# A decode kernel (cached attention plus a ReLU feed-forward) whose two last products are turned: activations stationary in four column tiles of the array, output stored as rows

## The chip, the cores and the metric

One core of one Trainium2 chip. The metric is the device time of one execution in microseconds (us); each kernel is run several times, and compared with runs of the kernel before made in the same sitting. "Faster", "same" and "slower" have a line at 2%.

TensorE multiplies matrices, VectorE and ScalarE work on vectors, GpSimd fills and copies small things, SyncE here only issues transfers. In the profile they are PE (PEld for weight loads), DVE, ACT, POOL and SP; a trailing q (SPq, ACTq) is the sequencer of that engine, where the issues of transfers stand.

## The reference

```python
# x [2,1,512]; k_cache, v_cache [2,32,8192,128]; wq [512,4096]; wo [4096,512]
# w1 [512,1792]; w2 [1792,512]; all bf16
xn  = layernorm(x)
q   = (xn @ wq), 32 heads of 128
p   = softmax(q k^T / sqrt(128)) over the 8192 cached keys
att = (p v, heads joined) @ wo
ffn = max(xn @ w1, 0) @ w2
out = x + att + ffn                      # [2,1,512]
```

The caches are 2 x 32 x 8192 x 128 x 2 bytes = 134 MB each. Two rows of 512 numbers come out. There is little to compute and much to read.

## The kernel before

The loop runs over 32 pairs of heads: keys are transposed on TensorE, scores and weighted sums follow, and transfers of the next keys and values wait for the buffers to come free. The change leaves that loop alone. It concerns FFN2 (the product with w2, ahead of the loop), wo and the end. First the views of the accumulators:

```python
y = Sc[1][0:Bsz, :]                                      # FFN2: 2 x 512
fin = ot[0][:, 0:KT * Bsz].rearrange("p (b c) -> p c b", c=KT)   # 128 x (2 x 4)
```

TensorE computes `out = lhsT.T @ rhs`; `lhsT` is stationary and is loaded first, `rhs` moves through. FFN2 has the hidden activations stationary (two columns) and streams 512 columns of w2:

```python
for j in range(FJ):                                      # 16
    half = slice(0, HP if j >= FA else P)
    i = pe.matmul(y, lhsT=hT[half, j, :], rhs=w2_sb[half, j, :],
                  start=(j == 0), stop=(j == FJ - 1))
...
v.tensor_tensor(out=ys[:], in0=y, in1=xsb[:], op=ALU.add)   # FFN2 + x
```

After the loop, x + FFN2 is put into the accumulator `fin` by four small fp32 matmuls; wo then has its weights stationary, 128 x 128 at a time, and two moving columns. The result lies transposed (features on partitions), so it is cast, transposed on TensorE, copied and stored as eight adjacent rows of 128:

```python
for k in range(KT):
    pe.matmul(fin[:, k, :], lhsT=ys[:, k * P:(k + 1) * P], rhs=ident2[:],
              start=(k == 0), stop=False)
... # last pair, normalisation, OX = attention output in the order of wo
for c in range(NC):                                      # wo arrives in five pieces
    pe.wait_ge(dW[c], 16)
    for j in range(cuts[c], cuts[c + 1]):                # 32 in all
        for k in range(KT):                              # 4
            t = pe.matmul(fin[:, k, :], lhsT=wo_sb[:, j, k * P:(k + 1) * P],
                          rhs=OX[:, j, :], ...)
pe.transpose(tp[1][0:Bsz * KT, 0, :], yT[:]..., identb[:])
...
v.tensor_copy(yT[:], ...)                                # ahead of the transpose
v.tensor_copy(osb[:], tp[1][0:Bsz * KT, 0, :])           # behind it
sp.dma_start(out.rearrange("b s (c p) -> (b s c) p", p=P), osb[:])
```

## Time and profile before

| | before |
|---|---|
| time | 661.26 us, median of 3 runs (661.19 to 661.27) |
| span of the profiled run | 659.3 us |
| bytes read | 280.5 MB, 425 GB/s over the span |
| last piece of wo has landed | 655.54 us |
| store issued | 656.76 us |

A piece of wo has landed when the last increment of its semaphore has arrived (a semaphore is the counter that tells when a transfer is complete). The span counts from the first to the last instruction. Times in the views are us from its start. A row of the timeline has the start, the duration, the engine, the line, the operation, output<-input, the shapes and a count; the bracket at the end says how long the engine had stood idle and what ended that. The last part of the chain of work that ended last, with start, duration and piece, shows where the transfers stop being the limit:

```profile
625.89 29.65 DMA w_sb<-in_A_wo_dram
655.54 0.05 issue
655.58 0.39 PE ot L412 x8
655.97 0.02 issue
655.99 0.18 DVE yT L519
656.17 0.04 issue
656.21 0.28 PE tp L421
```

Until 655.54 us the chain is one long transfer; all that computation can lengthen or shorten at this end are the steps below it.

### The profile page before, as it was taken

The page shows a single profiled execution, that of the slowest core. Times are in us where ns is not written, and L with a number is a line of the kernel's source. Part 1 is how long each engine was busy: PE and PEld are TensorE (multiplying, and loading weights), DVE is VectorE, ACT ScalarE, POOL GpSimd, SP SyncE. Part 2 cuts the span into 40 slices and gives each one's busy share as a digit, 9 for nine tenths or more (in the row PEclk, how much of TensorE's full clock was granted, in tenths as well). Part 3 has the DMA queues.
Part 4 walks back from the last instruction along what each step waited for, and adds up shares of the span by engine and source line. Part 5 has one row for each costly group of instructions (what it writes and reads, how often), then busy time and mean ns, then how long its engine had stood idle before and what let it go on. Part 6 is the DMA issues. An engine that isn't in the chain of part 4 may idle for free.

```text
span 659.3 us, 26888 instructions
## 1 busy us (share of the span) xinstructions
PE 562.9 (85%) x12747; PEld 538.3 (82%) x12747; DVE 253.4 (38%) x437; ACT 255.9 (39%) x403; POOL 9.0 (1%) x46
## 2 busy tenths in 40 slices
PE   2998899988799787889888788979787998788796
PEld 0488898988799787888888788978787988788795
DVE  1054344433344343334434334434333444334341
ACT  1043444444334433344343434434243444334340
POOL 1000000000000000000000000000000000000000
PEclk9798899989989898999889899979899989889998
DMA  8999999999999999999999999999999999999996
GB/s 363 447 417 437 419 437 429 431 439 423 439 423 435 431 429 439 423 439 423 435 435 427 441 419 439 427 431 437 425 441 419 439 427 431 437 425 441 421 426 266
DMA packets 10670, 280.66 MB, mean 426 GB/s; under 512 B 1250, under 2 KB 1252, under 8 KB 1828
## 3 DMA queue, kind: packets, MB, share of 16 engines
q1 hardware_dynamic: 10656, 280.50, 99.1%
q8 instruction: 9, 0.15, 0.1%
q14 instruction: 1, 0.01, 0.0%
q10 hardware_dynamic: 4, 0.00, 0.0%
HBM read 280.50 MB, written 0.00 MB: 425 GB/s over the span
## 4 chain that ended last, share of the span: by engine, by line
DMA 56%; PE 39%; ACT 2%; issue 1%; SPq 0%; DVE 0%; ACTq 0%
DMA ks<-in_A_k_cache_dram 50%; PE tp L300 21%; PE Sc L307 11%; DMA w_sb<-in_A_wo_dram 4%; PE ot L320 4%; DMA vs<-in_A_wq_dram 2%; ACT kT L427 2%; PE ot L252 1%; PE Sc L285 1%; PE ot L266 1%; ACT L427 1%; SPq L199 0%; PE Sc L355 0%; PE Sc L358 0%; SPq L194 0%
## 5 line engine op out<-in xcount | busy, mean ns | idle before, releaser
L300 PE MATMUL tp<-identb,ks 128*128 128x128 bf16 x4096 | 326.0, 229 | 68.2 <-DMA ks<-in_A_k_cache_dram 67.4
L427 DVE COPY kT<-tp 128x1024 bf16<-128x1024 bf16 x320 | 219.8, 691 | 325.1 <-PE tp L300 324.9
L300 PEld LDWEIGHTS tp<-identb,ks 128*128 128x128 bf16 x4096 | 257.2, 103 | 72.1 <-DMA ks<-in_A_k_cache_dram 70.5
L427 ACT COPY kT<-tp 128x1024 bf16<-128x1024 bf16 x192 | 194.3, 1012 | 233.4 <-PE tp L300 233.4
L307 PE MATMUL Sc<-q,kT 128*128 128x64 bf16 x4096 | 216.6, 196 | 4.6 <-ACT kT L427 4.6
L307 PEld LDWEIGHTS Sc<-q,kT 128*128 128x128 bf16 x4096 | 178.8, 100 | 7.9 <-ACT kT L427 7.8
L320 PE MATMUL ot<-prm,vs 128*128 128x64 bf16 x4224 | 156.1, 192 | 4.7 <-issue 4.7
L320 PEld LDWEIGHTS ot<-prm,vs 128*128 128x128 bf16 x4224 | 139.0, 97 | 7.5 <-issue 4.9
L542 ACT COPY nm<-Sc 128x2 f32<-128x2 f32 x32 | 5.1, 160 | 118.4 <-PE Sc L358 118.4
L546 ACT ACTIVATE prm<-Sc,nm 64x128 bf16<-64x128 f32 x64 | 25.6, 401 | 4.3
L483 DVE TENSOR_REDUCE mcol<-Sc 64x1 bf16<-64x128 f32 x64 | 18.6, 291 | 17.6 <-PE Sc L307 17.2
L427 ACT ACT_TABLE_LOAD x16 | 20.5, 1283 | 2.2
L252 PE MATMUL ot<-vs,xz 128*16 128x512 bf16 x32 | 9.3, 462 | 8.8 <-DMA vs<-in_A_wq_dram 8.8
L534 ACT COPY OTf<-ot 128x2 f32 x32 | 5.1, 160 | 27.3 <-PE ot L320 27.3
L488 DVE TENSOR_REDUCE mx<-Sc 1x2 bf16<-1x128 bf16 x32 | 8.9, 279 | 16.9 <-PE Sc L355 16.9
L252 PEld LDWEIGHTS ot<-vs,xz 128*16 128x16 bf16 x32 | 3.3, 103 | 14.4 <-issue 12.0
L237 POOL COPY q<-qb 128x2 bf16<-128x2 bf16 x32 | 5.9, 187 | 590.8 <-PE Sc L307 567.5
L546 ACT ACTIVATION_READ_ACCUMULATOR prm<-Sc,nm x64 | 11.8, 185 | 0.0
L457 DVE TENSOR_SCALAR qs<-ot 16x512 bf16<-16x512 f32 x1 | 0.7, 678 | 17.9 <-PE ot L252 17.9
L355 PE MATMUL Sc<-identb,mcol 128*1 128x128 bf16 x32 | 7.0, 217 | 0.0
L285 PE MATMUL Sc<-w_sb,hT 128*2 128x512 bf16 (+1 forms) x16 | 6.0, 544 | 0.1
L358 PE MATMUL Sc<-mx,onesb 1*128 1x2 bf16 x32 | 5.5, 172 | 0.0
(56 smaller groups left out, 38.6 us busy)
## 6 DMA issues: line engine op xcount, KB each, us to landing
ks<-in_A_k_cache_dram SPq DMA_DIRECT2D x32, 4096.0 KB, 26.7
vs<-in_A_v_cache_dram SPq DMA_DIRECT2D x31, 4096.0 KB, 31.3
vs<-in_A_wq_dram SPq DMA_DIRECT2D x1, 4096.0 KB, 12.3
vs<-in_A_v_cache_dram SPq DMA_DIRECT2D x2, 2048.0 KB, 20.0
w_sb<-in_B_w_dram SPq DMA_DIRECT2D x1, 1792.0 KB, 16.1
w_sb<-in_A_wo_dram SPq DMA_DIRECT2D x1, 1792.0 KB, 26.0
w_sb<-in_B_w_dram SPq DMA_DIRECT2D x1, 1536.0 KB, 19.3
w_sb<-in_A_wo_dram SPq DMA_DIRECT2D x1, 896.0 KB, 27.7
```

The source lines that it names most:

```text
L237: g.tensor_copy(q2[t % R][:], qb[:, 2 * t:2 * t + 2]).then_inc(sQ1, 1)
L252: i = pe.matmul(qp, lhsT=xz[:, kt, Z - g * Bsz:Z - g * Bsz + QG * Bsz], rhs=vs[1][:, (kt * QG + g) * 512:(kt * QG + g + 1) * 512], start=( ...
L266: i = pe.matmul(hp[0:HP if j >= FA else P, j, :], lhsT=w1_b[:, kt, j - FA, :] if j >= FA else w1_a[:, kt, j, :], rhs=xz[:, kt, Z:Z + Bsz], ...
L285: i = pe.matmul(y, lhsT=hT[half, j, :], rhs=w2_sb[half, j, :], start=(j == 0), stop=(j == FJ - 1),)
L300: t = pe.transpose(tp[e % 4][:, i, :], ks[r][:, kk * Dh:(kk + 1) * Dh], identb[:])
L307: t = pe.matmul(Sc[r][:, 2 * kk:2 * kk + 2 * REP], lhsT=kT[e % 4][:, i, :], rhs=rep(q2[r][:]), start=True, stop=True,)
L320: t = pe.matmul(ot[r][:, 0:2 * REP], lhsT=vs[r][:, kk * Dh:(kk + 1) * Dh], rhs=rep(prm[r][:, kk, :]), start=(kk == 0), stop=(kk == KB - 1),)
L355: pe.transpose(tr_of(r), mcol[r][:], identb[:]).then_inc(sT, 1)
L427: fn(kT[e % 4][:], tp[e % 4][:]).then_inc(kR[e], 1)
L483: m = v.tensor_reduce(out=mcol[i][half, :], in_=S_of(i)[half, :, u], axis=AX.X, op=ALU.max)
L488: v.tensor_reduce(out=mx[i][:], in_=tr_of(i).rearrange("o (u m) -> o u m", u=2), axis=AX.X, op=ALU.max, negate=True,).then_inc(sX, 1)
L546: x = a.activation(out=prm[i][half, :, u], in_=S_of(i)[half, :, u], func=ACTF.Exp, bias=nm[i][half, u:u + 1], scale=1.0, accum_out=RS[half ...
```

## The change

The intent is to use the array better with only two activation rows. The activations, padded with zeros to 32 columns, become stationary; the weights move. The 128 columns of the array are used as four column tiles of 32, each of which takes its own quarter of the 512 output columns, so four matmuls can be in the array at once. The output then lies as rows: batch b, quarter c on partition 32c + b. The transpose and its two copies go, one addition remains, and the store becomes two stores of four rows, each 32 partitions from the next.

```diff
-    y = Sc[1][0:Bsz, :]
-    fin = ot[0][:, 0:KT * Bsz].rearrange("p (b c) -> p c b", c=KT)
+    y = Sc[1][:, 0:P]
+    fin = ot[0][:, 0:P]
+    def cols(ap, c):
+        return ap[c * CT:(c + 1) * CT, :]                # CT = 32
+    out_v = out.rearrange("b s (c p) -> (b s) c p", p=P)
+    def store(eng, b):
+        eng.dma_start(out_v[b], osb[b:b + (KT - 1) * CT + 1:CT, :]).then_inc(dO, 16)
 ...                                       # FFN2
-            i = pe.matmul(y, lhsT=hT[half, j, :], rhs=w2_sb[half, j, :], ...)
+            for c in range(KT):
+                pe.matmul(cols(y, c), lhsT=hT[half, j, :],
+                          rhs=w2_sb[half, j, c * P:(c + 1) * P], ...)
+        for c in range(KT):                # x joins by an identity
+            i = pe.matmul(cols(y, c), lhsT=identb[0:Bsz, 0:CT],
+                          rhs=xsb[:, c * P:(c + 1) * P], ...)
 ...                                       # after the loop
-        for k in range(KT):
-            pe.matmul(fin[:, k, :], lhsT=ys[:, k * P:(k + 1) * P], rhs=ident2[:], ...)
 ...                                       # wo
-                    t = pe.matmul(fin[:, k, :], lhsT=wo_sb[:, j, k * P:(k + 1) * P],
-                                  rhs=OX[:, j, :], ...)
+                    t = pe.matmul(cols(fin, k), lhsT=OX[:, j, :],
+                                  rhs=wo_sb[:, j, k * P:(k + 1) * P], ...)
-        pe.transpose(tp[1][0:Bsz * KT, 0, :], yT[:]..., identb[:])
 ...                                       # VectorE
-        v.tensor_copy(yT[:], ...)
-        v.tensor_copy(osb[:], tp[1][0:Bsz * KT, 0, :])
+        v.tensor_tensor(out=osb[:], in0=fin, in1=ys[:], op=ALU.add)
 ...                                       # SyncE, then ScalarE
-        sp.dma_start(out.rearrange("b s (c p) -> (b s c) p", p=P), osb[:])
+        store(sp, 0)
+        a.wait_ge(sE, 1)
+        for b in range(1, Bsz):
+            store(a, b)
```

Cut here: `OX` and `hT` become 32 columns wide and are zeroed at the start by GpSimd and VectorE.

## The prediction

> **What bounds the kernel now.** I read the page first: busy shares, the slices, then the bytes.
>
> ```profile
> PE 562.9 (85%) x12747; PEld 538.3 (82%) x12747; DVE 253.4 (38%) x437; ACT 255.9 (39%) x403; POOL 9.0 (1%) x46
> ...
> DMA  8999999999999999999999999999999999999996
> GB/s 363 447 417 437 419 437 429 431 439 423 439 423 435 431 429 439 423 439 423 435 435 427 441 419 439 427 431 437 425 441 419 439 427 431 437 425 441 421 426 266
> ...
> HBM read 280.50 MB, written 0.00 MB: 425 GB/s over the span
> ```
>
> The DMA row is at nine tenths in every slice but the first and last, and the GB/s row stands between 417 and 447 in between. TensorE looks busy (85%), but the view of waits says who waits for whom:
>
> ```profile
> PE tp L300 <- DMA ks<-in_A_k_cache_dram: 67.4, 26, 3.4
> ```
>
> In 26 of the 32 steps over a pair of heads TensorE waits for its block of keys, 67.4 us in all. So the loop is bound by 280.5 MB of reads, which the change does not touch; 280.5 MB over about 430 GB/s is an estimate of 652 us of transfer. What a change of arithmetic can reach is only (a) the end, after the last bytes have landed, and (b) the start, if TensorE became so late there that the transfers ran out of freed buffers. For (a) the timeline from 650.5 us on:
>
> ```profile
> 650.64 2.33 PEld L412 LDWEIGHTS ot<-OX,w_sb 128*128 128x128 bf16 x84 [0.44 <-DVE OX L515]
> 650.65 2.41 PE L412 MATMUL ot<-OX,w_sb 128*128 128x2 bf16 x84 [0.32 <-DVE OX L515]
> 654.09 0.71 PEld L412 LDWEIGHTS ot<-OX,w_sb 128*128 128x128 bf16 x24 [1.13 <-DMA w_sb<-in_A_wo_dram]
> ...
> 655.58 0.29 PEld L412 LDWEIGHTS ot<-OX,w_sb 128*128 128x128 bf16 x8 [0.18 <-DMA w_sb<-in_A_wo_dram]
> 655.99 0.17 DVE L519 CAST yT<-ot 128x8 bf16<-128x8 f32 x1 [5.40 <-PE ot L412]
> 656.21 0.08 PEld L421 LDWEIGHTS tp<-identb,yT 128*8 128x8 bf16 x1 [0.34 <-DVE yT L519]
> 656.21 0.27 PE L421 MATMUL tp<-identb,yT 128*8 128x128 bf16 x1 [0.26 <-DVE yT L519]
> 656.52 0.21 DVE L521 COPY osb<-tp 8x128 bf16<-8x128 bf16 x1 [0.36 <-PE tp L421]
> 656.76 0.32 SPq L201 DMA_DIRECT2D out_dram<-osb  x1
> ```
>
> Here 84 of the 128 matmuls of wo run at once, then TensorE waits for the later pieces of wo. The chain of the work that ended last has the last piece of wo landing at 655.54 us (its 29.65 us of DMA end there). After it come 0.39 us for the last eight matmuls, then cast, transpose, copy, and the store at 656.76; the span ends at 659.3. The path that the change can shorten is therefore 655.54 to 656.76, 1.22 us, plus whatever the store does in its last 2.54 us.
>
> **What the Trainium skill says.** "TensorEngine Tiling (Array Packing)", section Tiling Modes, says that different tiles load weights and multiply in parallel, and that a change of tiling mode drains the engine; its section Restrictions says that column tiling turns fast weight load off. No matmul of the kernel before writes fewer than all columns at an offset, so its trace neither confirms nor denies this. "TensorE: Matmul & The Clock Gate", section Part 3, gives 2.38 times for three column tiles of 32 columns with 512 moving columns. Its Part 1 has only two clocks on one core, half and full; this trace agrees: the stretches show 1.00 until 652 us and 0.50 from 653.1 to the end. "DMA: Bandwidth & Descriptors", section Issuing engines are not separate DMA queues, says that two issuing engines save only issue time; here that concerns the two small stores.
>
> **The change part by part.**
>
> FFN2, before: 16 matmuls with 512 moving columns took 5.96 us, from 27.06 to 33.02, at clock 0.50 (chain of waits and stretches). After: 64 matmuls plus 4 for x, each with 128 moving columns, cycling over four column tiles. Serial at half clock: the 631 ns form above starts every 427 ns (the weight loads stand at 27.44, 27.87, 28.30), so 128 columns cost a quarter, 107 ns, and 68 of them 7.3 us, 1.3 us more. With four at a time it is limited by issue; the wo stream before issued a weight load and a matmul every (2.41-0.164)/83 = 27 ns, so about 68 x 30 = 2 us, 4 us less. Neither reaches the end. Until 44.19 us the queue holds 4096+1792+1536+256+3x4096 KB = 20.4 MB; the stretches of 5 us give 1.1 MB up to 5 us and a mean of 434 GB/s from there, so at 44.19 us, when the next block of keys is issued, some 2.3 MB or 5.4 us of work are still queued. A start later by 1.3 us eats part of that slack; a start earlier by 4 us only lets TensorE wait longer for keys. I book 0.
>
> The bias matmuls for ys (8 instructions, 644.07 to 645.05, 1.05 us) go: x and FFN2 are now added by VectorE at the end. The weighted sums of the last pair started right after them without a wait, so the normalised output, and wo with it, should start about 1.0 us earlier, near 649.6 us. This is hidden: the later pieces of wo are waited for anyway. It gives slack of 1 us to a slower wo.
>
> The memsets of hT (VectorE) and OX (GpSimd) fall into idle time at the start: VectorE waited 0.83 us for x there, GpSimd 23 us for the queries. 0.
>
> wo: 128 matmuls as before, but the moving side is 128 columns of wo, the stationary one OX padded to 32 columns. With four tiles at a time and an issue of 27 to 35 ns, 84 take at most 84 x 35 = 2.9 us from 649.6, done by 652.5, before the next piece lands at 654.09. The last eight after 655.54: 7 x 27 = 0.19 us plus the latency of one of 128 columns at half clock, 0.27 (the transpose at 656.21, the same 128 columns), is 0.46 against 0.39: +0.07 us.
>
> The end: cast 0.18, hand-over 0.04, transpose 0.28, hand-over 0.02, copy 0.21, hand-over 0.03 make 0.76 us and go. In their place comes one VectorE add of 128x128 f32 from PSUM and SBUF. From this trace: such an add over 62 columns took 0.22 us, over 512 columns 0.68 us, so 1.02 ns a column, and 128 columns 0.29 us; with two hand-overs 0.34 us. Saved: 0.42 us.
>
> The store: one issue of 0.32 us for 8 rows on SyncE becomes two of 4 rows each, on SyncE and ScalarE at once. At the start of the kernel ScalarE's issue of a small load took 0.56 us beside 0.40 us for SyncE's, so I add 0.1 us (of the 0.16 us difference, some may hide).
>
> Sum on the path: +0.07 - 0.42 + 0.10 = about -0.25 to -0.35 us, taking the small terms as uncertain. 661.26 - 0.3 gives 660.96; I say **660.9**.
>
> **The rivals.**
>
> *Column tiles do not overlap in this stream.* For it: fast weight load is off, and each matmul carries 128 columns in place of 2, with a new weight load before each. Against it: the skill's factor, and the transposes here, which also load new weights each and stream 128 columns, start every (1.51-0.23)/23 = 56 ns at full clock, so the worst serial case is known. At 56 ns wo takes 84 x 0.056 = 4.7 us from 649.6, to 654.3, and the other 44 take 2.5 us, to 656.8, plus latency 0.2: 657.0 against 655.97, so +1.0 us, net of the shorter end +0.7: about 662.0. If the clock falls to half as it did at 653, 44 x 107 ns = 4.7 us and a part of the first 84 run at that pace: net +3.5 to +4.5, about 665. Both are still within 2%.
>
> *The end is limited by the store.* The 2.54 us from issue to the end stay; two completions must be counted, one from a ScalarE queue that was last used at 0.92 us. That could give back 0.3 us or more: 661.2 to 661.5.
>
> *The saving is real but drowned by transfers.* Slices of 419 to 447 GB/s show how uneven they are; one part in a thousand of 652 us is 0.65 us, twice my saving. The three runs before agree within 0.08 us, which speaks against a large effect of this kind between runs, but another program may settle differently by some tenths.
>
> *The start delays the transfers.* It would need over 5 us more at FFN2, and even the serial case gives 1.3 us.
>
> **Range and chances.** I give four tiles at a time about 0.75 (660.4 to 661.3), serial at mostly full clock 0.15 (661.5 to 662.5), serial at half clock 0.1 (663 to 666). So 8 in 10 lie from 660.3 to 662.6. Two per cent is 13 us: the whole stretch from the last landing to the end is 3.8 us, so faster by 13 us cannot come from this change; slower by 13 us would need even more than the serial half-clock case. Same: 0.98.
>
> **What would show it right or wrong.** The last landing of wo should stay near 655.5 us and the bytes the same. The matmuls of wo should be done with the first 84 before the second piece lands, with a mean start-to-start of 27 to 35 ns, and TensorE should show waits for wo as before; if there are none, the serial rival holds. From the last matmul to the store's issue should be about 0.35 us in place of 0.79. FFN2 should take about 2 us in place of 5.96, and the wait of TensorE for keys should grow by about what FFN2 saves, with the span unmoved by it. From the store's issue to the end should stay near 2.5 us. I am wrong if transfers change their pace, or if column tiles cost more than 107 ns each.

## The result, and the profile after

| | before | after |
|---|---|---|
| time, median of 5 runs | 661.27 us (661.19 to 661.34) | 661.93 us (661.57 to 663.03) |
| span of the profiled run | 659.3 us | 659.8 us |
| last piece of wo has landed | 655.54 us | 655.59 us |
| last matmul of wo done | 655.97 us | 656.07 us |
| store issued | 656.76 us | 656.41 us |
| from the issue to the end | 2.6 us | 3.4 us |

The ratio of after to before is 1.0012, with a 95% interval of 1.0000 to 1.0025: the same by the 2% line. A ratio is the mean time of one kernel's fast runs over that of the other's in the same rounds, so it is not quite the ratio of the medians. The time lies in the predicted range, 660.3 to 662.6, but on the other side of before: about 0.3 us less was expected and 0.66 us more came. The medians overstate the loss: two of the five runs after stand high (662.47 and 663.03), and a second set of five of the same kernel came out 0.29 us above before (e11). The traces put it at 0.40 us, as the table of the experiments shows.

First what did not move. The bandwidth row and the total of the page of the kernel after:

```profile
GB/s 361 442 419 439 423 435 429 429 439 429 435 429 429 437 425 439 427 433 429 429 441 427 435 429 429 439 423 439 427 433 433 425 443 425 435 429 429 439 418 257
...
HBM read 280.50 MB, written 0.00 MB: 425 GB/s over the span
```

The transfers are the same bytes at the same pace. Now the end, in the timeline of the kernel after:

```profile
649.34 0.23 DVE L516 CAST OX<-Sc 128x64 bf16<-128x64 f32 x1 [0.38 <-PE Sc L400]
...
650.10 1.16 PE L414 MATMUL ot<-w_sb,OX 128*32 128x128 bf16 x56 [0.80 <-DMA w_sb<-in_A_wo_dram]
...
652.19 0.57 PE L414 MATMUL ot<-w_sb,OX 128*32 128x128 bf16 x28 [0.93 <-DMA w_sb<-in_A_wo_dram]
...
654.07 1.97 PE L414 MATMUL ot<-w_sb,OX 128*32 128x128 bf16 x44 [1.31 <-DMA w_sb<-in_A_wo_dram]
...
656.10 0.29 DVE L520 TENSOR_TENSOR osb<-ot,ys 128x128 bf16<-128x128 f32 x1 [6.53 <-PE ot L414]
656.41 0.58 SPq L168 DMA_DIRECT2D out_dram<-osb  x1
656.42 0.60 ACTq L168 DMA_DIRECT2D out_dram<-osb  x1
```

The reader sees three things. OX is ready at 649.57 us, a microsecond before its time in the kernel before, and nothing comes of it: wo waits for its first, second and third pieces. The matmuls themselves are quick: 28 of them take 0.57 us. The end is short: cast, transpose and copy are gone. But the last two rows, the issues of the stores, last 0.58 and 0.60 us, where the single store before lasted 0.32.

The trace also keeps the single packets of a transfer and the increments of its semaphore; no view prints them, so they were read from the packed trace. In the kernel before the store's first packet started 0.79 us after the issue had begun, and its last increment arrived after 1.19 us. In the kernel after SyncE's first packet started after 1.22 us, ScalarE's after 1.58 us, and the last increment arrived after 1.99 us. From the last increment to the end of the span it was 1.39 us before and 1.38 us after. So the sum is: landing of wo +0.05, last eight matmuls +0.05, from there to the issue -0.45 (0.79 to 0.34), from the issue to the last increment +0.80, rest -0.01; together +0.44, the difference of the spans (659.3 to 659.8) to within the rounding. **The shorter end was gained as predicted, and the store took more than that back.**

At the start, the timeline of the kernel after:

```profile
27.23 2.02 PE L287 MATMUL Sc<-w_sb,hT 128*32 128x128 bf16 x64
...
29.18 0.29 PE L295 MATMUL Sc<-xsb,identb 2*32 2x128 bf16 x4
...
32.31 2.74 PE L310 MATMUL tp<-identb,ks 128*128 128x128 bf16 x24 [2.84 <-DMA ks<-in_A_k_cache_dram]
```

The same stretch before:

```profile
27.06 5.96 PE L285 MATMUL Sc<-w_sb,hT 128*2 128x512 bf16 x16
32.95 1.51 PE L300 MATMUL tp<-identb,ks 128*128 128x128 bf16 x24
```

FFN2 is done at 29.47 in place of 33.02 us, and TensorE then waits 2.84 us for the first keys.

### The profile page after: what moved, and what is told of

The parts are those of the page before. It is cut to its first block, busy times and chain, and to the rows that moved or that the text cites. A ratio compares the mean times of both kernels' runs of the same rounds, so it can differ in the third digit from the quotient of the medians.

```text
span 659.8 us, 26975 instructions
## 1 busy us (share of the span) xinstructions
PE 556.1 (84%) x12790; PEld 534.7 (81%) x12790; DVE 253.8 (38%) x437; ACT 255.8 (39%) x403; POOL 9.5 (1%) x45
## 4 chain that ended last, share of the span: by engine, by line
DMA 61%; PE 34%; ACT 2%; issue 2%; SPq 1%; DVE 0%; ACTq 0%
DMA ks<-in_A_k_cache_dram 56%; PE tp L310 21%; PE Sc L317 10%; DMA w_sb<-in_A_wo_dram 5%; PE ot L330 3%; ACT kT L425 1%; SPq L190 1%; ACT L425 0%; SPq L207 0%; PE Sc L365 0%; SPq L202 0%; PE Sc L368 0%; PE ot L414 0%; SPq L183 0%; SPq L182 0%
## 5 line engine op out<-in xcount | busy, mean ns | idle before, releaser
L414 PE MATMUL ot<-w_sb,OX 128*32 128x128 bf16 x128 | 3.5, 250 | 3.3 <-DMA w_sb<-in_A_wo_dram 3.0
L414 PEld LDWEIGHTS ot<-w_sb,OX 128*32 128x32 bf16 x128 | 2.2, 107 | 4.4 <-DMA w_sb<-in_A_wo_dram 3.3
```

Of the source, the lines that this page charges most:

```text
L414: t = pe.matmul(cols(fin, k), lhsT=OX[:, j, :], rhs=wo_sb[:, j, k * P:(k + 1) * P], start=(j == 0), stop=(j == WJ - 1),)
```

## The experiments

Each kernel was run five times for time, and profiled. The medians of the kernel before lie between 661.27 and 661.30 us in all sittings. What the trace shows of the stores of all of them is gathered here; "first bytes" and "last increment" are counted from the beginning of the first issue. The column "landing to end" runs from the landing of the last piece of wo to the end of the profiled span. It is the cleanest measure of the end, because that landing itself came anywhere from 655.34 to 655.59 us, and runs of the same form agree in it within 0.02 us (after, e6, e11; before, e7; e1, e4; e9, e12).

| run | stores | issues, us | first bytes, us | last increment, us | landing to end, us | median, us (range) |
|---|---|---|---|---|---|---|
| before | 8 adjacent rows, SyncE | 0.32 | 0.79 | 1.19 | 3.80 | 661.27 (661.19 to 661.34) |
| after | 4 + 4 rows, step 32, SyncE and ScalarE | 0.58, 0.60 | 1.22, 1.58 | 1.99 | 4.20 | 661.93 (661.57 to 663.03) |
| e1 | 8 adjacent rows, SyncE | 0.32 | 0.80 | 1.20 | 3.40 | 660.89 (660.58 to 662.34) |
| e2 | 4 + 4 rows, step 32, SyncE twice | 0.58, 0.52 | 1.22, 1.78 | 2.19 | 4.39 | 661.92 (661.54 to 663.60) |
| e3 (kernel before) | 4 + 4 adjacent rows, SyncE and ScalarE | 0.30, 0.27 | 0.78, 0.76 | 1.34 | 3.96 | 661.44 (661.32 to 661.83) |
| e4 | 8 adjacent rows, ScalarE | 0.30 | 0.78 | 1.19 | 3.39 | 660.88 (660.64 to 660.97) |
| e5 | 8 rows, step 2, SyncE | 0.68 | 1.32 | 1.73 | 3.93 | 661.36 (661.23 to 663.00) |
| e6 (FFN2 undone) | as after | 0.58, 0.60 | 1.22, 1.58 | 1.99 | 4.19 | 661.83 (661.72 to 662.09) |
| e7 (FFN2 alone) | as before | 0.32 | 0.79 | 1.20 | 3.80 | 661.41 (661.18 to 661.69) |
| e8 | 4 + 4 adjacent rows, two steps in the output | 0.68, 0.73 | 1.33, 1.69 | 2.05 | 4.26 | 661.84 (661.74 to 663.35) |
| e9 | 4 stores of 2 adjacent rows | 0.29, 0.31; 0.25, 0.28 | 0.73 to 1.15 | 1.62 | 3.82 | 661.58 (661.28 to 663.06) |
| e10 | as e8, one step in the output | 0.30, 0.27 | 0.80, 0.78 | 1.35 | 3.55 | 661.18 (660.98 to 662.33) |
| e11 (after again) | as after | 0.58, 0.60 | 1.22, 1.58 | 1.98 | 4.18 | 661.57 (661.33 to 661.92) |
| e12 (FFN2 undone) | as e9 | 0.29, 0.31; 0.25, 0.28 | 0.74 to 1.15 | 1.63 | 3.83 | 661.22 (661.07 to 661.40) |

The first theory (T in the expectations) was that two engines which issue at the same moment hinder each other. Rivals were the form of the store (S), ScalarE's queue (A) and the loop (L).

### e1: the store of before in the changed kernel (wrong result)

```diff
-        eng.dma_start(out_v[b], osb[b:b + (KT - 1) * CT + 1:CT, :])
+        eng.dma_start(out_v, osb[0:Bsz * KT, :])      # out_v: "(b s c) p"; SyncE only
```

> The changed kernel, but with the store of the kernel before: one transfer of the eight adjacent rows 0 to 7, issued by SyncE alone. The result is wrong on purpose (rows 2 to 7 are padding), the work is the same. Theory T (the lost time is the store's: two engines issue at once, each issue takes 0.58 to 0.60 us in place of 0.32, and the last bytes land 1.99 us after the issue in place of 1.19): issue near 656.4 us lasting 0.32 us, span 2.54 us after it, so about 658.9, and a time of 660.9 (0.35 us under before). Rival L (the loop or the start became slower or more uneven): time stays near 661.9 and the spread of 661.6 to 663.0 stays.

Measured: 660.89 us, one run at 662.34; the span of the profiled run is 658.7 us. The store's row, with the shortest, median and longest issue in ns:

```profile
L168 SPq DMA_DIRECT2D out_dram<-osb x1: 323/323/323, 656.2 to 656.2; - x1
```

Everything but the store is as in the kernel after, and the time falls by 1.04 us, to the number that had been predicted for the whole change. Not all of that is the store: the profiled spans differ by 1.05 us, of which 0.25 is an earlier landing of wo (655.34 against 655.59), and 0.80 is the store. The store's part alone is more than the whole loss, so the loss sits in the stores. This does not yet say what about them: e1 has both one issuer and adjacent rows.

### e2: both stores from SyncE

```diff
-        store(sp, 0)
+        for b in range(Bsz):
+            store(sp, b)
```

(and none from ScalarE)

> The changed kernel with both stores of four rows issued by SyncE, one after the other; correct result. Theory T (contention of two engines issuing at once): each issue takes about 0.32 us, the second starts at 656.75, so the end is about 0.37 us later than with one store: span 659.3, time about 661.3. Rival S (the rows at a distance of 32 partitions make the store slow): the issues still take near 0.58 us each, the second is done at 657.6, span 660 or more, time 662 or more. Rival L: 661.9 with the wide spread.

```profile
L168 SPq DMA_DIRECT2D out_dram<-osb x2: 515/548/582, 656.3 to 656.9; - x2
```

Measured: 661.92 us. With a single issuer the issues still last 0.58 and 0.52 us. Theory T falls on its own number (0.32 us, 661.3). Rival S had 0.58 us, a span of 660 or more and 662 or more; the issues are as it said, and span (659.8) and time come close.

### e3: the kernel before with its store split between two engines

```diff
-        sp.dma_start(out.rearrange("b s (c p) -> (b s c) p", p=P), osb[:])
+        store(sp, 0)                    # rows 0 to 3
...
+        a.wait_ge(sE, 1)
+        store(a, 1)                     # rows 4 to 7
```

> The kernel before, with nothing changed but the store: four adjacent rows issued by SyncE and four by ScalarE at once; correct result. Theory T: both issues take near 0.6 us, the end comes 0.8 us later, span 660.1, time about 662.1. Rival S: nothing changes (661.3), since the rows are adjacent. Rival L: nothing changes, 661.3.

```profile
L165 SPq DMA_DIRECT2D out_dram<-osb x1: 302/302/302, 656.6 to 656.6; - x1
L165 ACTq DMA_DIRECT2D out_dram<-osb x1: 274/274/274, 656.6 to 656.6; - x1
```

Measured: 661.44 us, 0.16 above the kernel before of the same sitting. Two engines that issue adjacent rows at once keep their short issues, and the first bytes of both start within 0.02 us of one another. T falls a second time; it had said 662.1.

### e4: one store, from ScalarE (wrong result)

```diff
-        store(sp, 0)
...
-        for b in range(1, Bsz):
-            store(a, b)
+        store(a)                        # eight adjacent rows, as e1
```

> The changed kernel with one store of eight adjacent rows issued by ScalarE alone (wrong result on purpose). Theory T: no second issuer, so as e1, near 660.9 to 661.0. Rival A (it is ScalarE's queue that is slow, having rested since the start): later than e1 by 0.4 us or more, 661.3 to 661.9.

Measured: 660.88 us, as e1. ScalarE's queue is as good as SyncE's, although it had rested for 655 us. Rival A falls.

### e5: every second partition (wrong result)

```diff
-        eng.dma_start(out_v, osb[0:Bsz * KT, :])
+        eng.dma_start(out_v, osb[0:2 * Bsz * KT - 1:2, :])
```

> As the run with one store of eight adjacent rows on SyncE (660.89 us, issue 0.32 us, first bytes 0.80 us after the issue), but the eight rows are taken from every second partition (0, 2, ..., 14). Wrong result on purpose. Theory S (a source whose partitions are not adjacent makes the issue itself slow, whatever the number of issuers): issue 0.55 us or more and first bytes 1.2 us or more after it; time 661.3 or more. Rival D (only the large distance of 32, over all four quarters of the partitions, is slow): as with adjacent rows, 0.32 us and 660.9.

```profile
L168 SPq DMA_DIRECT2D out_dram<-osb x1: 682/682/682, 656.3 to 656.3; - x1
```

Measured: 661.36 us, 0.47 above e1, from a step of 2 in place of 1. From landing to end it is 0.53 us more. The distance of 32 is not needed: with rows at a step of 2 the issue itself is about twice as long, and the first bytes come 0.52 us later. The kernel before had long issues of a like form to show, in the loads of the last rows of w2, eight transfers of eight rows at a partition step of 4, at the very start:

```profile
L182 SPq DMA_DIRECT2D w_sb<-in_B_w_dram x8: 623/623/797, 2.4 to 7.2; - x8
L174 SPq DMA_DIRECT2D w_sb<-in_B_w_dram x1: 402/402/402, 1.4 to 1.4; - x1
```

The second row is a load of 128 adjacent partitions, sixteen times the rows, and its issue takes 0.40 us. These are loads, issued back to back, so they suggest the rule and do not test it.

### e6: the change without FFN2

```diff
-            for c in range(KT):
-                pe.matmul(cols(y, c), ...)
+            i = pe.matmul(y, lhsT=hT[half, j, :], rhs=w2_sb[half, j, :], ...)
...
+        for k in range(KT):             # x + FFN2, fp32, ahead of wo
+            pe.matmul(cols(fin, k), lhsT=idw[:], rhs=ys[:, k * P:(k + 1) * P], ...)
```

> The changed kernel with FFN2 as before (16 matmuls with 512 moving columns, the sum of x and FFN2 added by four fp32 matmuls before wo); wo in column tiles and the two stores of rows at distance 32 stay. Correct result. Theory S (all of the loss is the store's): near 661.9 as the changed kernel. Rival L (the earlier start of the loop costs something, and makes the runs of 662.3 to 663.6): median lower by some tenths and no run above 662.2.

Measured: 661.83 us, issues of 0.58 and 0.60 us. The loss is there without the new FFN2.

### e7: FFN2 alone in the kernel before

```diff
+            for c in range(KT):
+                pe.matmul(cols(y, c), lhsT=hT[half, j, :],
+                          rhs=w2_sb[half, j, c * P:(c + 1) * P], ...)
...
-            pe.matmul(fin[:, k, :], lhsT=ys[:, k * P:(k + 1) * P], rhs=ident2[:], ...)
+            pe.matmul(fin[:, k, :], lhsT=ys[:], rhs=pick[:, k, :], ...)
```

> The kernel before with FFN2 alone in column tiles (about 2.2 us in place of 5.96, so TensorE is ready for the keys near 29.5 us in place of 33); wo, its transpose and its store as before. Correct result. Theory S: as before, 661.2 to 661.4, since the transfers never wait for FFN2. Rival L: slower by some tenths, or single runs 1 to 2 us above the others.

Measured: 661.41 us; ratio to before 1.0002, interval 0.9988 to 1.0015. What TensorE saves it waits for, as the timeline shows:

```profile
29.02 0.29 PE L295 MATMUL Sc<-xsb,identb 2*32 2x128 bf16 x4
32.49 0.93 PE L310 MATMUL tp<-identb,ks 128*128 128x128 bf16 x7 [3.18 <-DMA ks<-in_A_k_cache_dram]
```

### e8: rows on adjacent partitions, a version meant to beat both

A zero-padded stationary operand leaves free on which partition of its 32 a row comes out. With the two useful columns last in tiles 0 and 2 and first in tiles 1 and 3, the rows lie on partitions 30 to 33 and 94 to 97.

```diff
-                        lhsT=OX[:, j, :],
+                        lhsT=OX[:, j, win(k)],     # 32 of 62 columns, by parity of k
...
+        top = (2 * h + 1) * CT
+        eng.dma_start(out_v[2 * h:2 * h + 2], osb[top - Bsz:top + Bsz, :])
```

> The changed kernel, correct result, with the two useful columns of the padded stationary operand put last in column tiles 0 and 2 and first in tiles 1 and 3, so that the rows come out on partitions 30 to 33 and 94 to 97: two stores of four adjacent rows, on SyncE and ScalarE. Theory S: issues near 0.3 us, as in the run of the kernel before with two such stores, which cost 0.16 us over one store; so 660.89 + 0.16, about 661.05, under both kernels. Rival D or any rival that blames two issuers together with column tiles: 661.5 or more.

```profile
L175 SPq DMA_DIRECT2D out_dram<-osb x1: 675/675/675, 656.3 to 656.3; - x1
L175 ACTq DMA_DIRECT2D out_dram<-osb x1: 728/728/728, 656.3 to 656.3; - x1
```

Measured: 661.84 us. A clear miss: adjacent partitions, and the issues are longer than ever. But the rows come in the order (quarter, batch), so the addresses in the output run with two steps, 512 numbers and 128. Theory P followed: an issue is short where the rows are adjacent *and* each side has only one step from row to row.

### e9: four stores of two adjacent rows

```diff
-        store(sp, 0)
+        for c in range(KT // 2):
+            store(sp, c)                # out[:, c], osb[32c : 32c + 2]
...
+        for c in range(KT // 2, KT):
+            store(a, c)
```

> The changed kernel, correct result, with four stores of two adjacent rows each (one for each column tile), two on SyncE and two on ScalarE. Theory P (an issue is fast where the rows are adjacent and each side has one row step, slow otherwise): each issue near 0.30 us; the second of each engine starts 0.33 us after the first, first bytes of the last near 0.33 + 0.8 us after the first issue; so 660.89 + 0.16 + 0.33, about 661.4, 0.5 us under the changed kernel and level with before. Rival N (more stores cost more, whatever their form): 662 or more.

```profile
L168 SPq DMA_DIRECT2D out_dram<-osb x2: 286/300/313, 656.3 to 656.6; - x2
L168 ACTq DMA_DIRECT2D out_dram<-osb x2: 252/264/277, 656.3 to 656.5; - x2
```

The trace is as P had it: four short issues, with one step of 512 numbers in the output, and the last increment after 1.62 us in place of 1.99. The time is inconclusive: three runs at 661.28 to 661.58, and two at 662.28 and 663.06, so that the median, 661.58, is no better than that of the changed kernel in the same sitting (e11, 661.57). From landing to end the profiled runs differ clearly, 3.82 against 4.18 us.

### e10: e8 with one step in the output (wrong result)

```diff
-    out_v = out.rearrange("b s (c p) -> c (b s) p", p=P)
+    out_v = out.rearrange("b s (c p) -> (b s c) p", p=P)
```

> The run with rows on partitions 30 to 33 and 94 to 97 again (its issues took 0.675 and 0.728 us, median 661.84), but each store writes four consecutive rows of the output, so the destination has one row step. Wrong result on purpose. Theory P: issues near 0.30 us, 661.0 to 661.1. Rival B (it is the source that crosses from one group of 32 partitions to the next, or starts at 30): still 0.67 to 0.73 us and 661.8.

```profile
L175 SPq DMA_DIRECT2D out_dram<-osb x1: 303/303/303, 656.4 to 656.4; - x1
L175 ACTq DMA_DIRECT2D out_dram<-osb x1: 274/274/274, 656.4 to 656.4; - x1
```

Measured: 661.18 us, against 661.84 for e8. The source is the same to the byte, so neither the start at partition 30 nor the crossing from one group of 32 to the next matters: it was the destination with two steps. (e8 differs from e10 in one thing more: its stores show two 4-byte packets each, which carry the increments, in place of four. That is not the cause, since the stores of e9 show two as well and have short issues.)

### e11: the changed kernel once more

> The changed kernel once more, unaltered. Theory P: median 661.7 to 662.0 and issues of 0.58 and 0.60 us. For the open point of single slower runs: of 30 runs of kernels with both parts of the change, 7 stood 1.1 to 1.8 us above the others' level; if that belongs to these kernels, about one in five of these runs does so again; if it belonged to the chip at those moments, none.

Measured: 661.57 us, just under the 661.7 to 662.0 that were expected, and 0.29 above before in that sitting, where the first sitting had 0.66; none of the five runs stood out. The issues and the last increment are as the first time. Between sittings a kernel's median can thus move by some tenths, and differences of 0.2 us rest on the traces more than on the times.

### e12: plain stores, FFN2 as before

> The run with FFN2 as before and wo in column tiles (661.83 us, no run above 662.1), with the four plain stores of two adjacent rows in place of the two stores of rows at distance 32; correct result. Theory P: issues of 0.25 to 0.31 us, the last bytes landing about 1.6 us after the first issue in place of 1.99, so about 661.4, level with before (661.28). For the open point of single slower runs: with both parts of the change 10 of 45 runs stood more than 1 us above their kernel's fastest; with FFN2 undone, or FFN2 alone, none of 10. If the early start of the loop after the short FFN2 is needed for them, none here; if wo and the stores are enough, about one of five.

The edit joins those of e6 and e9. Measured: 661.22 us (661.07 to 661.40), correct, against 661.30 for before in the same sitting: ratio 0.9997, interval 0.9984 to 1.0011. Against e6 (661.83), which differs in the stores alone, it is 0.6 us less. Of all correct kernels with the turned wo this is the best, level with the kernel before; no correct kernel here is shown to beat it. The 660.9 us of e1 and e4 need the eight rows on adjacent partitions in output order, which column tiles do not give. A single transfer for all eight rows of the turned wo was not tried.

### What stays open

Some runs stand far above the others of the same kernel. Counted at 0.9 us or more above the kernel's own fastest run, it was 10 of the 45 runs, in nine sets of five, with both the turned wo and the turned FFN2 (two of "after", e8 and e9; one of e1, e2, e5, e10; none of e4, e11), and none of 20 of e3, e6, e7 and e12, nor of the runs of the kernel before. (The expectations of e11 and e12 put the line for these counts loosely, at "1.1" and "more than 1 us"; strictly above 1 us there are 8.) Their spans are longer too (661.1 and 660.4 us in the two of "after", against 659.6 to 659.8), so the time is lost inside the kernel. No profile fell on such a run. What was argued, not shown: the first keys after the start are released later with the short FFN2. In the timelines SyncE issued the third block of keys at 44.19 us before and at 45.18 us after, the fourth at 64.97 and 66.11 us. The queue then holds work until about 69 us (an estimate: 28.8 MB issued by then, 18.5 MB moved by 45 us, 434 GB/s), so the slack is 4 us before and 3 after. A run in which TensorE comes a few us later still would let the transfers run dry. In the profiled runs they never did (no inner slice of any page is under 413 GB/s). e7 has the short FFN2 too and showed no such run, but five runs are too few: at 10 in 45 a set of five has none more than one time in four.

The rule on the form of a store has been tried on small stores alone, and one load does not fit it: ScalarE's load of x at the start, two adjacent rows, took 0.56 us to issue in the kernel before, beside SyncE's issue of 0.40. No run here tells why. Nor does any run have a single slow store on ScalarE, so whether the 0.36 us by which its first bytes came after SyncE's is due to the other store is not shown.

## Why the prediction was right or wrong

**Bound by transfers; only the two ends matter: right.** Same bytes, same GB/s, last landing 655.54 and 655.59 us.

**Column tiles work four at a time: right, and faster than priced.** The starts of the matmuls in the trace come in groups of four within 8 to 23 ns; the groups start every 56 ns at full clock and every 107 ns at half clock, exactly the time of 128 moving columns. That is 14 and 27 ns a matmul, where 27 to 35 was predicted. The last eight took 0.44 us (predicted 0.46). The serial rival is out.

**FFN2: right in size, with a turn that was missed.** It took 2.24 us (predicted 2), and TensorE waited 2.84 us for keys. But it waited at half clock, and the first transposes ran so: 310 ns each in place of 219, and in this pair of profiles the first pair's key buffer was released a microsecond later than before, not earlier. That cost nothing in the profiled run (e7: 661.41).

**wo a microsecond earlier, hidden: right.** OX was ready 1.02 us earlier, and TensorE then waited 0.80 us for the first piece of wo. One reading was off: the row of 84 matmuls in the profile before had looked like one run, yet it held a gap where the second piece begins, as the starts show (56 matmuls, a gap of 0.16 us at 652.04, 28 more). The 27 ns that the prediction took from this row include that wait; the starts are 25 ns apart. A merged row can hide a short wait inside it.

**The end, -0.42 us: right.** Measured -0.45; the addition took 0.29 us as worked out.

**The store, +0.10 us: this is the term that failed.** It measured +0.80 us from issue to last increment, and from the issue to the end 3.37 us against 2.58 before, where the prediction had named "near 2.5 us" as a sign of being right (its 2.54 comes of a rounded span). With the store of before (e1) the end is 0.80 us shorter. The prediction looked at *who* issues, and took the 0.16 us between two issues at the start of the kernel. It did not look at *what* is issued: rows at a partition step of 32. The rows with a step of 4 in the same profile, 0.62 us each, were in the view that had been read for the weights. Priced by them, the term would have been about +0.3 and the sum about zero. The rest, another 0.13 us to the first bytes and 0.36 us by which ScalarE's first bytes came after SyncE's, I found in no row of the profile before. The rival "the end is limited by the store" was named, with the right direction, 661.2 to 661.5, and for the wrong reason, the idle queue of ScalarE, which e4 clears.

That the range held is luck: it was made wide for another rival, the serial column tiles, which did not occur. The case that did occur, four tiles at a time, had been given 660.4 to 661.3, and 661.93 lies outside it, on the other side of before. A small slip besides: the terms add to -0.25 us, which gives 661.0 and not 660.9. And the zeroing of OX, booked as falling into idle time, did hold up VectorE at the start (the last point below), at no cost to the time.

## What to carry to other kernels

Where a kernel is bound by its reads, a change of arithmetic at the end is worth only what lies between the last landing and the last store, so price that stretch to the tenth of a microsecond, the store included. These small stores were paid by their form: adjacent partitions with one step on each side were issued in 0.3 us and gave first bytes after 0.7 to 0.8 us; a partition step, or two steps in the destination, made that 0.5 to 0.7 and 1.2 to 1.3 us, and of two such stores issued at once the second's first bytes came another 0.36 us later. A layout that saves a transpose may hand the store a worse form; look for a row of the same form in the profile at hand before pricing it.

## What the Trainium skill lacked or had wrong

- "DMA: Bandwidth & Descriptors": its section on issuing engines has only the sequencer's issue time to save with two engines. The runs add that the issue depends on the form: 0.25 to 0.32 us for 2 to 8 adjacent rows, 0.52 to 0.60 us for four rows at a step of 32, 0.68 us for eight at a step of 2, 0.68 to 0.73 us for a destination with two steps. I found this on no page.
- "Perfetto Trace Analysis", section DMA Instruction — HWDGE, has the sequencers share one block for descriptors, locked while one uses it. The slow forms would fit that (the second engine's first bytes 0.36 us after the first's), though ScalarE's recorded issue, 0.60 us beside SyncE's 0.58, does not contain such a wait; short forms show little of it (0.02 us in e3 and e10, 0.10 us in e9). Whether the lock is the cause, and which of the page's steps grows with the form, no run shows.
- "TensorE: Matmul & The Clock Gate", Part 3, says in its list of what overlaps that weight loads overlap matmuls in flight only where the row groups differ, though a sentence just above it allows for a background weight buffer too. Here four column tiles share all rows, each matmul has its own load, and the groups of four still start every 56 and 107 ns, the pace of a single stream of 128 columns (the transposes before: 56 ns); the loads are hidden, so the list's "only" does not hold here. Its 4 ns from tile to tile is confirmed (0 to 7 ns from neighbour to neighbour in most groups).
- "SBUF — State Buffer", section Who interferes with whom, says that VectorE in some of its modes and GpSimd share a pair of ports, which the first to come holds for its whole instruction while the other waits. The runs fit that: VectorE's scaling of x, a tensor_scalar, took 0.54 us before, 1.22 us beside the new memset of OX on GpSimd (0.96 us), and 2.04 us beside the wider one of e8 (1.76 us); both times it ended 0.27 us after the memset. It lay off the path here.
